# B step of a two-layer-type kernel: token rows of the queries turned by transposing DMAs, TensorE turning only the memory queries

## The chip, the core and the metric

One NeuronCore of one Trainium2 chip. The metric is the device time of one execution in microseconds (us), the time of that core. The kernel before was run three times: 2582.91, 2586.01 and 2589.53 us, median 2586.01 us.

## What is computed

Four residual layers run one after the other on a sequence of 2048 tokens of width 640: A, B, A, B, with a layer norm ahead of each. A is a segmented attention with a compressive memory and is not touched by the change. B is a recurrent attention with a memory of 8 rows, and its 64 segments of 32 tokens must be done in order, since the memory of a segment is what the segment before gave out:

```
mem = mem0                                             # 8 rows of 640
for s in range(64):                                    # segments of 32 tokens
    h = concat([mem, x[32*s : 32*s+32]])               # 40 rows
    q, k, v = h@Wq, h@Wk, h@Wv                         # 32 heads of 128
    scores = q@k.T / sqrt(128)                         # per head, 40 x 40
    scores = where((row < 8) | (row >= col), scores, -1e9)
    o = softmax(scores)@v @ Wo                         # 40 rows of 640
    mem = o[:8];  outs.append(o[8:])
```

## The kernel before, in words

A B layer is a loop of 64 steps (line 1089), one for each segment, with a setup ahead of it (lines 988 to 1038). All numbers in bf16, sums in fp32 in PSUM (the accumulation memory behind TensorE, which ScalarE and VectorE empty into SBUF).

**Which rows a step handles.** A step s projects 32 columns at once: the 8 memory rows of segment s, which have just been made by step s-1, and 24 token rows of segment s+1, which are known long before. So each of the projections gives 8 columns that are needed at once (by the scores of step s) and 24 that are kept for the next step. The other 8 token rows of a segment ("tails") are projected ahead in units of their own (`tail_unit`, `vtail_unit`), go through DRAM (`b_QKd`, `b_VTd`) and come back by DMA.

**The order of a step.** Every engine's order is written out by hand: `_OrdNC` (line 119) chains the instructions of TensorE, ScalarE, VectorE and GpSimd in the order of the program text. DMAs are issued by SyncE (SP), whose queue is in order too. The tile framework adds the semaphores: an instruction waits for whoever wrote what it reads, and for the readers and writers of the buffer that it takes over. In a step:

1. `thin_mm` (line 879) makes Ka, Qa, Kb, Qb: 16 heads each, 20 products, in PSUM as 128 rows (4 groups of heads by 32 columns) by 512. `kq` (line 1108) copies each to SBUF as bf16: Ka, Kb and Qb by ScalarE, Qa by VectorE (lines 1164 to 1171). The queries are scaled by SCB on the way.
2. These have to be turned, so that a head's 128 numbers lie along partitions. `transp4` (line 888) turns one 128 x 512 block by four TensorE transposes of 128 columns into a PSUM tile: TPak, TPaq, TPbk, TPbq (lines 1173 to 1183).
3. `scatter` (line 895) takes the 8 memory columns of each block by VectorE into this step's KT and QT, and `x_scatter` (line 1104) the 24 token columns by ScalarE into the next step's KT and QT. So VectorE does four copies of 128 x 128 and ScalarE four of 128 x 384.
4. `mask_mm` lays the mask into the score tiles SPa (ahead of TPbq) and SPb (behind it); `scores` (line 1119) then adds the products of 16 heads into SPa and of 16 into SPb, first with QT (the weights) and then with QZ (the tails' queries).
5. Softmax: row maxima, subtraction, sums and the normalization by VectorE (one half by GpSimd), exponentials by ScalarE; VectorE turns the probabilities (`p_turn`).
6. Beside the softmax TensorE makes Va, Vb and one tail unit; then the probability products (`pv`, tile b_OTP), the output projection (b_OPS, and a deferred part b_OPSd), a tail unit of V, and the eight new memory rows (b_MT) that VectorE puts into the next step's columns b_HX.

SyncE issues in a step two stores and two loads of the residual rows (b_XO, lines 1052 and 1102), a store of the tail unit (line 941), four loads of V tails (line 917), two stores of V tails (line 970), and in some steps a load of tails (line 907), of a layer norm's rows (line 848), and stores and loads of the deferred rows (lines 1061 and 1063).

In QT a head's 32 columns lie together: `QT[s][:, h, :]`, tokens first (0 to 23), memory rows last (24 to 31). The masks (`build_masks`, line 172) and the selection of the memory rows (`selm`) follow that order. The buffers b_kq (4) and b_QT (2) are used in turn.

Of the kernel before, what the change touches and what calls it, by code (L numbers as in the profile page):

```python
# [18 lines left out]
F32 = mybir.dt.float32  # L19
BF16 = mybir.dt.bfloat16  # L20
ACT = mybir.ActivationFunctionType
ALU = mybir.AluOpType
# [148 lines left out]

def build_masks(G, C, pool):

    G.tensor_tensor(out=C.selm[:, 0, :], in0=C.identb[:, 24:32], in1=C.identb[:, 88:96], op=ALU.add)
    G.tensor_tensor(out=C.selm[:, 1, :], in0=C.identb[:, 56:64], in1=C.identb[:, 120:128], op=ALU.add)
    G.memset(C.keep[:], 3e38)
    G.affine_select(out=C.keep[:], in_=C.keep[:], pattern=[[1, 128]], compare_op=ALU.is_ge, fill=0.0, base=0, channel_multiplier=-1)
    negs = pool.tile([128, 32], F32, name="b_negs", tag="am")
    G.memset(negs[:], -1e9)
    maskf = pool.tile([128, 2, 40], F32, name="b_maskf", tag="am")  # L180
    G.memset(maskf[:], 0.0)

    def above(out, rows, ncol, base, chan, colstep=1):
        G.affine_select(out=out, in_=negs[rows, 0:ncol], pattern=[[colstep, ncol]], compare_op=ALU.is_gt,
                        fill=0.0, base=base, channel_multiplier=chan)

    for i in range(4):
        r32 = slice(32 * i, 32 * i + 32)
        for k in (3, 2, 1, 0):
            rk = slice(32 * i, 32 * i + 8 * k + 8)  # L190
            above(maskf[rk, 0, 0:8], rk, 8, 8 * k, -1)
        above(maskf[r32, 1, 8:32], r32, 24, 0, -1)
        above(maskf[r32, 1, 0:8], r32, 8, 24, -1, 0)
    G.tensor_copy(C.mask5[:, 0, :], maskf[:, 0, :])
    G.tensor_copy(C.mask5[:, 1:5, :], maskf[:, 1, :].unsqueeze(1).to_broadcast([128, 4, 40]))

# [49 lines left out]
def layer_A(nc, tc, C, W, x_src, x_dst, src_is_bf16, nseg=4, out_bf16=False, xb_dst=None, load_w=None, side_loads=None):  # L246
# [7 lines left out]
    with ExitStack() as ctx:  # L254
# [367 lines left out]
        if src_is_bf16:  # L622
            build_masks(P, C, up)
# [154 lines left out]
def layer_B(nc, tc, C, W, x_src, xb_src, x_dst, mem0, B_Wv, B_Wo, nsteps=64, out_bf16=False, tag=""):  # L778
    SCB = 1.0 / math.sqrt(128.0)
    nc_raw = nc  # L780
    nc = _OrdNC(tc, nc_raw, engines=ORDER_ENGINES)
# [5 lines left out]
    with ExitStack() as ctx:  # L787
        def pool(name, bufs):
            return ctx.enter_context(tc.tile_pool(name=name, bufs=bufs, reuse_waits="tile"))
# [89 lines left out]
        def thin_mm(cols_ap, Wt, b, name):  # L879
            ps = ps_tile([128, 512], F32, name)  # L880
            for c in range(NCH):
                for j in range(4):
                    n = 4 * b + j
                    nc.tensor.matmul(ps[32 * j:32 * j + 32, :], lhsT=cols_ap[:, c, :], rhs=Wt[:, c, 512 * n:512 * n + 512],
                                     start=(c == 0), stop=(c == NCH - 1), tile_position=(0, 32 * j), skip_group_check=True)
            return ps

        def transp4(sb, name, tp=None):
            if tp is None:
                tp = ps_tile([128, 4, 128], BF16, name)  # L890
            for i in range(4):
                nc.tensor.transpose(tp[:, i, :], sb[:, 128 * i:128 * i + 128], C.identb[:])
            return tp

        def scatter(eng, tp, b, dst_t, t0, t1, c0):
            src = tp[:].rearrange("p i (j t) -> p i j t", j=4)[:, :, :, t0:t1]
            dst = dst_t[:, 16 * b:16 * b + 16, c0:c0 + (t1 - t0)].rearrange("p (j i) c -> p i j c", j=4)
            evac(eng, dst, src)

        def alloc_seg(s):  # L900
            QT[s] = w2.tile([128, 32, 32], BF16, name="b_QT", tag="QT")
            KT[s] = w2.tile([128, 32, 40], BF16, name="b_KT", tag="KT")

        def tails_load(s):
# [70 lines left out]
        def d_half(rows, jj2):  # L975
            return rows.rearrange("t (c j x) -> t j c x", j=2, x=64)[:, jj2]
# [36 lines left out]
        for nm, b in jobs:  # L1013
            ps = thin_mm(cols, W.wk if nm == "K" else W.wq, b, f"b_{nm}p")
            sb = kqp.tile([128, 512], BF16, name="b_kq", tag="kq")
# [4 lines left out]
        alloc_seg(0)  # L1020
        for (nm, b), sb in zip(jobs, sbs):
            tp = transp4(sb, "b_TP")
            scatter("dve" if nm == "K" else "act", tp, b, KT[0] if nm == "K" else QT[0], 8, 32, 8 if nm == "K" else 0)
        entered.append(1)
        XO, XOd = init_state()
        tl = tails_load(0)
# [22 lines left out]
        def store_head(s):  # L1049
            def f(xo):  # L1050
                for jj2 in range(2):
                    nc.sync.dma_start(d_half(x_dst[32 * s:32 * s + 24, :], jj2), xo[32 * jj2:32 * jj2 + 24, :].rearrange("t (c x) -> t c x", x=64))
            return f

        def tail_dma(s0, store, xo):
# [33 lines left out]
        for s in range(nsteps):  # L1089
            last = (s == nsteps - 1)  # L1090
# [8 lines left out]
                if s % 2:  # L1099
                    tl = tails_load(s + 1)  # L1100
            for jj2 in range(2):
                nc.sync.dma_start(XO[32 * jj2:32 * jj2 + 24, :].rearrange("t (c x) -> t c x", x=64), d_half(x_src[32 * s:32 * s + 24, :], jj2))

            def x_scatter(tp, b, D_):
                if not last:
                    scatter("act", tp, b, D_[s + 1], 8, 32, 8 if D_ is KT else 0)

            def kq(ps, eng, scale=None):
                sb = kqp.tile([128, 512], BF16, name="b_kq", tag="kq")
                evac(eng, sb[:], ps[:], scale)  # L1110
                return sb

            def mask_mm(b):
                SP = ps_tile([128, 5, 40], F32, f"b_SP{b}")
                nc.tensor.matmul(SP[:].rearrange("p g k -> p (g k)"), lhsT=C.identb[:], rhs=mask5[:].rearrange("p g k -> p (g k)"),
                                 start=True, stop=False, skip_group_check=True)
                return SP

            def scores(SPs):
                qz = QZ[:].rearrange("p h c -> p (h c)")  # L1120
                for b in range(2):
                    for tail in range(2):
                        for i in range(4):
                            for j in range(4):
                                h = 16 * b + 4 * j + i
                                lhsT = qz[:, 32 * h - 8 * i:32 * h - 8 * i + 32] if tail else QT[s][:, h, :]
                                nc.tensor.matmul(SPs[b][32 * j:32 * j + 32, 0 if tail else 1 + i, :], lhsT=lhsT, rhs=KT[s][:, h, :],
                                                 start=False, stop=True, tile_position=(0, 32 * j), skip_group_check=True)

# [37 lines left out]
            qa = kq(Qa, "dve", SCB)  # L1167
            Kb = thin_mm(cols, W.wk, 1, "b_Kb")
            kb = kq(Kb, "act")
            Qb = thin_mm(cols, W.wq, 1, "b_Qb")  # L1170
            qb = kq(Qb, "act", SCB)

            TPak = transp4(ka, "b_TPak")
            scatter("dve", TPak, 0, KT[s], 0, 8, 32)
            x_scatter(TPak, 0, KT)
            TPaq = transp4(qa, "b_TPaq")
            scatter("dve", TPaq, 0, QT[s], 0, 8, 24)
            x_scatter(TPaq, 0, QT)
            TPbk = transp4(kb, "b_TPbk")
            scatter("dve", TPbk, 1, KT[s], 0, 8, 32)  # L1180
            x_scatter(TPbk, 1, KT)
            SPa = mask_mm(0)
            TPbq = transp4(qb, "b_TPbq", po.tile([128, 4, 128], BF16, name="b_TPbq", tag="tail"))
            scatter("dve", TPbq, 1, QT[s], 0, 8, 24)
            x_scatter(TPbq, 1, QT)
            SPb = mask_mm(1)
            scores((SPa, SPb))
            for f in (soft_max, soft_sub, soft_exp):
# [59 lines left out]
            if not last:  # L1248
# [130 lines left out]
```

## Time and profile before

The profile is of one more execution.

| what | number |
|---|---|
| median of 3 runs | 2586.01 us |
| profiled execution, its own time | 2585.25 us |
| its span (first to last instruction) | 2583.5 us |
| granted TensorE clock over the span | 0.996 |
| a B step, from its first product of Ka to the next step's: median in the first B layer, in the second | 13.99, 13.97 us |
| shortest steps of both | 13.79 to 13.82 us |
| busy between 700 and 800 us of the span (first B layer): PE, PEld, DVE, ACT, POOL | 99.57, 64.95, 58.42, 52.09, 12.86 us |
| SP: time of its DMA issues in a step, mean of 56 steps of the first B layer | 9.76 us |

PE is TensorE's products, PEld its weight loads, DVE VectorE, ACT ScalarE, POOL GpSimd, SP SyncE's queue. A row of the timeline has the start in us from the span's start, the time in us, the engine, the line, the operation, the tiles (out<-in), the shape and how many were merged; in brackets the idle time ahead of it and what ended it. Nearly all rows of a B step carry line 109, since the helper that records the order makes the call; they are told apart by their tiles. A PE row's end is modelled, and the rows overlap, so that a PE that looks busy can still have waited.

### The profile page before, as it was taken

To read this page: it belongs to the slowest core of one execution; us is meant where nothing else is said; L and a number is where in the kernel's file an instruction comes from. 1 tells how busy PE (TensorE), PEld (TensorE's weight loads), DVE (VectorE), ACT (ScalarE), POOL (GpSimd) and SP (SyncE) were. 2 spreads that over 40 slices of the span, in tenths; PEclk is the share of its full clock that TensorE was granted. 3 is DMA by queue.
4 is the path that set the end of the run, shared out by engine and by line. 5 is a ranking of instruction groups with operands and counts; after the bars stand their busy time and mean duration, and the time that the engine had idled before them with its cause. 6 is when DMAs were issued, how large, how long until landed. Compare 5 with 4: busy or idle time off the path is not lost.

```text
span 2583.5 us, 139561 instructions
## 1 busy us (share of the span) xinstructions
PE 2482.8 (96%) x62024; PEld 1637.5 (63%) x62088; DVE 1704.5 (66%) x4738; ACT 1521.3 (59%) x3430; POOL 704.9 (27%) x1515
## 2 busy tenths in 40 slices
PE   7999999999999999999979899999999999999998
PEld 5556576666666666666655566766666666666665
DVE  8999855565556555555579998555655565565555
ACT  6988945555555545444369889455555555555443
POOL 6677621111111111111146776211111111111110
PEclk9999999999999999999999999999999999999999
DMA  4122272222222222121220112822212122211111
GB/s 158 45 84 73 83 245 51 48 47 46 46 50 48 46 50 43 40 39 30 61 85 17 63 50 55 265 47 47 44 42 47 42 46 43 46 43 35 38 26 21
DMA packets 325309, 157.19 MB, mean 61 GB/s; under 512 B 244960, under 2 KB 309600, under 8 KB 322912
## 3 DMA queue, kind: packets, MB, share of 16 engines
q1 hardware_dynamic: 324704, 148.26, 22.1%
q8 instruction: 485, 7.95, 1.3%
q14 instruction: 120, 0.98, 0.1%
HBM read 96.46 MB, written 51.71 MB: 57 GB/s over the span
## 4 chain that ended last, share of the span: by engine, by line
PE 77%; DVE 14%; ACT 6%; issue 2%; DMA 1%; POOL 0%; SPq 0%; ACTq 0%; DVEq 0%; POOLq 0%
PE b_OPS L109 11%; DVE a_nm L138 6%; PE b_Ka L109 5%; PE b_Qb L109 5%; PE b_Kb L109 5%; PE b_Qa L109 5%; PE b_tail L109 5%; PE b_SP L109 4%; PE b_Va L109 4%; PE b_Vb L109 4%; PE b_vtail L109 3%; PE b_OPSd L109 3%; ACT a_PT L138 3%; PE b_OTP L109 3%; PE a_S L109 2%
## 5 line engine op out<-in xcount | busy, mean ns | idle before, releaser
L109 PEld LDWEIGHTS <-b_HX 128*32 128x32 bf16 x15360 | 428.7, 96 | 329.5 <-DVE b_HX L109 0.5
L109 POOL TENSOR_TENSOR b_Pn<-b_E,b_rs 128x200 bf16<-128x200 bf16 x128 | 78.2, 611 | 1334.4 <-PE b_Vb L109 893.7
L138 DVE TENSOR_REDUCE a_nm<-a_S 128x2 f32<-128x512 f32 (+3 forms) x512 | 395.0, 816 | 34.7 <-PE a_S L109 26.4
L138 ACT ACTIVATE a_PT<-a_T 128x1024 bf16<-128x1024 f32 (+1 forms) x384 | 344.3, 901 | 32.8 <-PE a_T L109 25.0
L109 PE MATMUL b_OPS<-b_wo,b_OTsb 128*32 128x320 bf16 x8192 | 302.4, 299 | 1.8 <-issue 0.8
L109 PEld LDWEIGHTS <-b_OTsb 128*32 128x32 bf16 x8192 | 204.4, 96 | 77.2 <-DVE b_OTsb L109 3.1
L138 POOL TENSOR_SCALAR_AFFINE_SELECT a_PT<-a_PT 128x256 bf16<-128x256 bf16 x380 | 188.6, 505 | 129.8 <-ACT a_PT L138 128.4
L109 DVE CAST b_HX<-b_MT 128x8 bf16<-128x8 f32 x372 | 63.9, 172 | 232.3 <-PE b_MT L109 226.6
L109 ACT CAST b_msb<-b_OPS 128x64 bf16<-128x64 f32 x378 | 69.4, 256 | 222.1 <-PE b_OPS L109 222.0
L109 ACT CAST b_kq<-b_Kb 128x512 bf16<-128x512 f32 x128 | 75.0, 586 | 200.4 <-PE b_Kb L109 200.4
L109 DVE COPY b_KT<-b_TPak 128x128 bf16<-128x128 bf16 x128 | 28.8, 225 | 228.1 <-PE b_TPak L109 228.1
L109 DVE TENSOR_SCALAR b_kq<-b_Qa 128x512 bf16<-128x512 f32 x128 | 88.6, 692 | 120.0 <-PE b_Qa L109 116.7
L109 PE MATMUL b_Va<-b_wv,b_HX 128*32 128x512 bf16 x2520 | 161.1, 380 | 0.0
L109 PE MATMUL b_Vb<-b_wv,b_HX 128*32 128x512 bf16 x2520 | 160.9, 379 | 0.0
L109 PEld LDWEIGHTS <-b_kq 128*128 128x128 bf16 x2080 | 116.8, 98 | 68.9 <-ACT b_kq L109 55.6
L109 PE MATMUL b_Ka<-b_wk,b_HX 128*32 128x512 bf16 x2520 | 158.3, 378 | 0.0
L109 PE MATMUL b_Qa<-b_wq,b_HX 128*32 128x512 bf16 x2520 | 158.2, 379 | 0.0
L109 PE MATMUL b_Qb<-b_wq,b_HX 128*32 128x512 bf16 x2520 | 158.2, 379 | 0.0
L109 PE MATMUL b_Kb<-b_wk,b_HX 128*32 128x512 bf16 x2520 | 158.2, 379 | 0.0
L109 DVE CAST b_OTsb<-b_OTP 128x160 bf16<-128x160 f32 (+1 forms) x384 | 131.0, 377 | 35.0 <-PE b_OTP L109 28.9
L109 PEld LDWEIGHTS <-c_identb 128*128 128x128 bf16 x1240 | 102.2, 98 | 60.1 <-issue 29.4
L109 ACT CAST b_kq<-b_Ka 128x512 bf16<-128x512 f32 x128 | 75.0, 586 | 108.8 <-PE b_Ka L109 108.8
(206 smaller groups left out, 5502.4 us busy)
## 6 DMA issues: line engine op xcount, KB each, us to landing
b_QKd<-b_tu SPq DMA_DIRECT2D x128, 128.0 KB
b_tl<-b_QKd SPq DMA_DIRECT2D x64, 256.0 KB
b_wv<-in_B_Wv_dram SPq DMA_DIRECT2D x10, 1024.0 KB
b_wo<-in_B_Wo_dram SPq DMA_DIRECT2D x16, 640.0 KB
b_Vth<-b_VTd SPq DMA_DIRECT2D x512, 16.0 KB
b_XO<-xres SPq DMA_DIRECT2D x256, 30.0 KB
b_VTd<-b_vt SPq DMA_DIRECT2D x224, 32.0 KB
b_xt<-xres_bf SPq DMA_DIRECT2D x40, 160.0 KB
```

The source lines that it names most:

```text
L109: r = f(*a, **k)
L138: r = f(*a, **k)
```

## The change

In a step, the 24 token rows of the queries no longer come from a TensorE transpose and a copy by ScalarE. Two transposing DMAs, issued by SyncE, turn all 128 x 512 of qa and of qb straight from b_kq into the next step's QT. TensorE turns only the 8 memory columns of each 32: `mem_turn` makes products with b_kq as weights and a strided view of the identity (4 runs of 8 columns, 32 columns a product) into fp32 PSUM, and VectorE copies these 128 x 128 numbers into this step's QT. ScalarE's two copies of the token queries go. Qb is emptied from PSUM in two halves, by ScalarE and by VectorE. QT's layout becomes `[128, 2, 4, 128]`, with the memory columns first in each 32; masks, selection and the partitions of the residual rows (8 to 31 in place of 0 to 23) follow. K stays as it was. The setup makes the first QT as before, in the new layout. In the last step there is no next QT and no DMA, but the halves and `mem_turn` stay.

```
+        def mem_turn(sb, b, name, tp=None):
+            if tp is None:
+                tp = ps_tile([128, 4, 32], F32, name)
+            for i in range(4):
+                nc.tensor.matmul(tp[:, i, :], lhsT=sb[:, 128 * i:128 * i + 128], rhs=C.identb[:].rearrange("p (j t) -> p j t", t=32)[:, :, 0:8],
+                                 start=True, stop=True, skip_group_check=True)
+            return tp
+
+        def q_cols(s, b, t0, t1):
+            return QT[s][:, b, :, :].rearrange("p i (j t) -> p i j t", t=32)[:, :, :, t0:t1]
...
-            QT[s] = w2.tile([128, 32, 32], BF16, name="b_QT", tag="QT")
+            QT[s] = w2.tile([128, 2, 4, 128], BF16, name="b_QT", tag="QT")
...
-                nc.sync.dma_start(XO[32 * jj2:32 * jj2 + 24, :].rearrange("t (c x) -> t c x", x=64), d_half(x_src[32 * s:32 * s + 24, :], jj2))
+                nc.sync.dma_start(XO[32 * jj2 + 8:32 * jj2 + 32, :].rearrange("t (c x) -> t c x", x=64), d_half(x_src[32 * s:32 * s + 24, :], jj2))
...
-                                lhsT = qz[:, 32 * h - 8 * i:32 * h - 8 * i + 32] if tail else QT[s][:, h, :]
+                                lhsT = qz[:, 32 * h - 8 * i:32 * h - 8 * i + 32] if tail else QT[s][:, b, i, 32 * j:32 * j + 32]
...
-            qb = kq(Qb, "act", SCB)
+            qb = kqp.tile([128, 512], BF16, name="b_kq", tag="kq")
+            evac("act", qb[:, 0:256], Qb[:, 0:256], SCB)
+            evac("dve", qb[:, 256:512], Qb[:, 256:512], SCB)
+            if not last:
+                for b, sb in ((0, qa), (1, qb)):
+                    nc.sync.dma_start_transpose(out=QT[s + 1][:, b, :, :], in_=sb[:])
...
-            TPaq = transp4(qa, "b_TPaq")
-            scatter("dve", TPaq, 0, QT[s], 0, 8, 24)
-            x_scatter(TPaq, 0, QT)
+            TPaq = mem_turn(qa, 0, "b_TPaq")
+            evac("dve", q_cols(s, 0, 0, 8), TPaq[:].rearrange("p i (j t) -> p i j t", t=8))
...
-            TPbq = transp4(qb, "b_TPbq", po.tile([128, 4, 128], BF16, name="b_TPbq", tag="tail"))
-            scatter("dve", TPbq, 1, QT[s], 0, 8, 24)
-            x_scatter(TPbq, 1, QT)
+            TPbq = mem_turn(qb, 1, "b_TPbq", po.tile([128, 4, 32], F32, name="b_TPbq", tag="tail"))
+            evac("dve", q_cols(s, 1, 0, 8), TPbq[:].rearrange("p i (j t) -> p i j t", t=8))
```

More of the change, by code (lines that the diff above doesn't have):

```diff
@@ L172, in build_masks @@
 def build_masks(G, C, pool):
-    G.tensor_tensor(out=C.selm[:, 0, :], in0=C.identb[:, 24:32], in1=C.identb[:, 88:96], op=ALU.add)
-    G.tensor_tensor(out=C.selm[:, 1, :], in0=C.identb[:, 56:64], in1=C.identb[:, 120:128], op=ALU.add)
+    G.tensor_tensor(out=C.selm[:, 0, :], in0=C.identb[:, 0:8], in1=C.identb[:, 64:72], op=ALU.add)
+    G.tensor_tensor(out=C.selm[:, 1, :], in0=C.identb[:, 32:40], in1=C.identb[:, 96:104], op=ALU.add)
     G.memset(C.keep[:], 3e38)
@@ L191, in build_masks @@
             above(maskf[rk, 0, 0:8], rk, 8, 8 * k, -1)
-        above(maskf[r32, 1, 8:32], r32, 24, 0, -1)
-        above(maskf[r32, 1, 0:8], r32, 8, 24, -1, 0)
+        above(maskf[r32, 1, 8:32], r32, 24, 8, -1)
+        G.memset(maskf[r32, 1, 0:8], -1e9)
+        G.memset(maskf[32 * i:32 * i + 8, 1, :], 0.0)
     G.tensor_copy(C.mask5[:, 0, :], maskf[:, 0, :])
@@ L1022, in layer_B @@
             tp = transp4(sb, "b_TP")
-            scatter("dve" if nm == "K" else "act", tp, b, KT[0] if nm == "K" else QT[0], 8, 32, 8 if nm == "K" else 0)
+            if nm == "K":
+                scatter("dve", tp, b, KT[0], 8, 32, 8)
+            else:
+                evac("act", q_cols(0, b, 8, 32), tp[:].rearrange("p i (j t) -> p i j t", t=32)[:, :, :, 8:32])
         entered.append(1)
@@ L1051, in f @@
                 for jj2 in range(2):
-                    nc.sync.dma_start(d_half(x_dst[32 * s:32 * s + 24, :], jj2), xo[32 * jj2:32 * jj2 + 24, :].rearrange("t (c x) -> t c x", x=64))
+                    nc.sync.dma_start(d_half(x_dst[32 * s:32 * s + 24, :], jj2), xo[32 * jj2 + 8:32 * jj2 + 32, :].rearrange("t (c x) -> t c x", x=64))
             return f
@@ L1101, in layer_B @@
             for jj2 in range(2):
-                nc.sync.dma_start(XO[32 * jj2:32 * jj2 + 24, :].rearrange("t (c x) -> t c x", x=64), d_half(x_src[32 * s:32 * s + 24, :], jj2))
+                nc.sync.dma_start(XO[32 * jj2 + 8:32 * jj2 + 32, :].rearrange("t (c x) -> t c x", x=64), d_half(x_src[32 * s:32 * s + 24, :], jj2))
             def x_scatter(tp, b, D_):
                 if not last:
-                    scatter("act", tp, b, D_[s + 1], 8, 32, 8 if D_ is KT else 0)
+                    scatter("act", tp, b, D_[s + 1], 8, 32, 8)
             def kq(ps, eng, scale=None):
```

## The prediction

> **What bounds the kernel now.** I read the page first: the busy shares and the chain of work that ended last.
>
> ```profile
> PE 2482.8 (96%) x62024; PEld 1637.5 (63%) x62088; DVE 1704.5 (66%) x4738; ACT 1521.3 (59%) x3430; POOL 704.9 (27%) x1515
> PE 77%; DVE 14%; ACT 6%; issue 2%; DMA 1%; POOL 0%; SPq 0%; ACTq 0%; DVEq 0%; POOLq 0%
> ```
>
> TensorE is the bound, so its saved columns look like time. But PE's ends are modelled, so I then read the timeline where the change sits: all engines, 814.9 to 817.3 us, a step of the first B layer.
>
> ```profile
> 815.09 0.40 PE L109 MATMUL b_TPak<-c_identb,b_kq 128*128 128x128 bf16 x4
> 815.27 0.60 ACT L109 ACTIVATE b_kq<-b_Qb 128x512 bf16<-128x512 f32 x1 [0.50 <-PE b_Qb L109]
> 815.33 0.39 PE L109 MATMUL b_TPaq<-c_identb,b_kq 128*128 128x128 bf16 x4
> 815.53 0.23 DVE L109 COPY b_KT<-b_TPak 128x128 bf16<-128x128 bf16 x1 [1.78 <-PE b_TPak L109]
> ...
> 815.75 0.22 DVE L109 COPY b_QT<-b_TPaq 128x128 bf16<-128x128 bf16 x1
> ...
> 815.93 0.40 PE L109 MATMUL b_TPbq<-c_identb,b_kq 128*128 128x128 bf16 x4
> 815.97 0.23 DVE L109 COPY b_KT<-b_TPbk 128x128 bf16<-128x128 bf16 x1
> ...
> 816.36 0.23 DVE L109 COPY b_QT<-b_TPbq 128x128 bf16<-128x128 bf16 x1 [0.16 <-PE b_TPbq L109]
> ...
> 816.64 0.28 PE L109 MATMUL b_SP<-b_KT,b_QT 128*32 128x40 bf16 x16
> ...
> 816.83 0.83 DVE L109 TENSOR_REDUCE b_negmax<-b_SP 128x5 f32<-128x200 f32 x2 [0.24 <-PE b_SP L109]
> ```
>
> Qb's last product ends at 815.16 (modelled), ScalarE starts to empty it 0.11 later and is done at 815.87; only then TPbq; VectorE's last copy ends at 816.585; 0.054 later (median of 128 steps) the second 16 heads' scores start. Behind them in PE's order stands Va (816.86), and VectorE's second row maximum waits for them too. So **the end of VectorE's fourth copy starts the rest of the step on both engines**; until then TensorE has idle time that the 96% hides. Steps are 13.98 us (median), the shortest 13.8; TensorE or the softmax ends later by turns, and a delay of that copy moves both.
>
> Last, the groups by shape, for VectorE over the span and for ScalarE from 400 to 1290 us (after the bar: busy us, mean ns of one).
>
> ```profile
> L109 DVE TENSOR_SCALAR b_kq<-b_Qa 128x512 bf16<-128x512 f32 x128 | 88.6, 692 | 120.0 <-PE b_Qa L109 116.7
> L109 DVE CAST b_OTsb<-b_OTP 128x160 bf16<-128x160 f32 x256 | 80.2, 325 | 35.0 <-PE b_OTP L109 28.9
> L109 DVE CAST b_HX<-b_MT 128x16 bf16<-128x16 f32 x248 | 43.2, 175 | 6.0 <-PE b_MT L109 0.4
> L109 DVE COPY b_QT<-b_TPbq 128x128 bf16<-128x128 bf16 x128 | 28.8, 225 | 20.6 <-PE b_TPbq L109 19.9
> L109 DVE CAST b_OTdef<-b_vtail 128x256 bf16<-128x256 f32 x8 | 3.4, 425 | 4.6 <-PE b_vtail L109 4.6
> L109 DVE COPY b_KT<-b_TP 128x384 bf16<-128x384 bf16 x4 | 1.2, 348 | 0.0
> ```
>
> ```profile
> L109 ACT ACTIVATE b_kq<-b_Qb 128x512 bf16<-128x512 f32 x63 | 37.6, 597 | 31.7 <-PE b_Qb L109 30.9 <-PE b_TPak L109 0.8
> L109 ACT CAST b_kq<-b_Kb 128x512 bf16<-128x512 f32 x63 | 36.9, 586 | 98.5 <-PE b_Kb L109 98.5
> L109 ACT CAST b_vt<-b_vtail 128x256 bf16<-128x256 f32 x55 | 20.5, 372 | 29.7 <-ACT b_msb L109 26.5 <-issue 2.2 <-PE b_vtail L109 0.9
> ```
>
> From PSUM VectorE takes 1.04 ns a column in fp32 (256 columns 425, 512 692) but 0.48 in bf16 (128 columns 225, 384 348).
>
> **The change part by part.**
>
> *Qb in two halves.* The diff reads as if ScalarE and VectorE ran side by side. The instruction order of the changed program says otherwise: VectorE's half waits for ScalarE's semaphore, at the count that ScalarE's half of the same step raises (same PSUM tile, same SBUF tile). So the halves run in turn. ScalarE: 372 for 256 columns, plus 11 that an ACTIVATE takes over a CAST (597 - 586), 0.383 us. Hand-over: 0.033 (ScalarE's exponential to VectorE's sum, median). VectorE: 0.425 (the fp32 row of 256 columns; at 512 the scaled form takes what a cast takes, 692). So qb is whole at 815.27 + 0.383 + 0.033 + 0.425 = 816.11, not 815.87. Worse, this half stands in VectorE's order **ahead of its four copies**, three of which ran while ScalarE still emptied Qb.
>
> *The four copies.* Two stay (K, 0.225 each). The two of the memory queries now read fp32: between 175 at 16 columns and 325 at 160, 128 columns give 0.292. No row has this exact form; the ends are 0.225 (what the bf16 copy took) and 0.325. I take 0.292. Together 1.034, back to back: from 816.11 to 817.145, against 816.585. **The delay is 0.56 us a step.** All that they read is ready: TPbq's last two products start at about 816.16, when the half is done, and end within 0.3, while VectorE comes to the copy at 816.85.
>
> *TensorE's narrower products.* Eight products of 128 columns at 0.056 each (0.225 from one group of four to the next) become 32 columns. The trace has no 128-row weights with so few columns. Bounds: no gain (the weight load sets the pace), or 0.009 each (32 b_OTP products in 0.30), so 0 to 0.38 us a step. I count 0: TensorE then waits for VectorE's copies, which cover it whole. If that cover were gone, the start of the scores would still be VectorE's, not TensorE's.
>
> *ScalarE's two copies* (0.484 and 0.509 us) go. I count 0: its next work, the exponential, waits for VectorE's subtraction (0.94 idle ahead of it in this step); that wait grows.
>
> *The transposing DMAs.* Their order in SP's queue: qa behind the two stores of b_XO and ahead of its loads, qb behind the loads, ahead of the tail store (L941) and the V tails' loads (L917). Two things wait for them: the next step's copies into b_kq and its scores. The former is due 13 us after the issue of qa's, so even late landings cost nothing there. Of the issue:
>
> ```profile
> L1102 SPq DMA_DIRECT2D b_XO<-xres x256: 762/782/4413, 381.3 to 2564.8; - x128
> ```
>
> ```profile
> L941 SPq DMA_DIRECT2D b_QKd<-b_tu x128: 319/373/2332, 359.2 to 2334.6; - x128
> ```
>
> No transposing DMA is in the trace. Ends: 0.32 (the store of 128 partitions, 128 KB, the same bytes), and 4.41 (the longest b_XO load, with a wait in it). I take 0.78, the median of the b_XO loads, which move short pieces as the transposes do. SP issues 9.76 us a step; with two it is 11.3 of 14.54. Cost 0 below 2.39 us each, (14.54 - 9.76)/2. What is moved back behind them by 1 to 2 us (tail store, V tails) is used in the next step, over 8 us later.
>
> [...]
>
> *The rest at 0*: masks (eight small GpSimd writes for four, once, beside layer A, where GpSimd has idle time; at most 2 us); QT's layout (the scores' weights are 32 adjoining columns as before); b_XO's partitions (same shapes).
>
> **The sum.** The halves and copies are in all 64 steps of both layers: 128 x 0.56 = 71.7. The profiled execution took 2585.25 (span 2583.5 and 1.75 around it), so 2656.9, forecast **2657 us** (+2.8%); the runs' median is 0.76 above that execution, which I leave.
>
> **The rivals.**
>
> *SP becomes the bound.* For it: SP is 70% full, and every step would wait for it once an issue takes over 2.39. At 4.41 a step is 9.76 + 8.82 = 18.58, 4.6 over now, in 126 steps 580: 3165 us. Against it: every clean issue row is under 0.9.
>
> *The halves do run side by side* (were the wait for an older count). VectorE starts at about 815.21 and ends its copies at 815.21 + 0.425 + 1.034 = 816.67, 0.085 late: +11 us, 2596. Against it: the count.
>
> *Not slower: side by side and short copies.* If VectorE empties its half beside ScalarE and its memory copies cost less than 0.25 each, the last copy comes earlier than now. At 0.225 it ends at 816.535, 0.05 early: -6 us, 2579. For it: 0.225 is this very copy's row. Against it: the count, and both fp32 rows. Above 0.25 it turns into the rival before.
>
> **How the numbers follow.** Forecast 0.83; SP bound 0.07; side by side 0.04; side by side with short copies 0.04 (no change: a measurement here tells 0.3%, 8 us, from none); 0.02 for a gain that I see no mechanism for. Slower 0.94, same 0.04, faster 0.02. Range: memory copies at 0.225 give 0.426 x 128 = 55, 2640; at 0.325, 80, 2665. Some steps may also wait for a transpose behind a full SP queue (the steps with deferred rows, one in four; 0.8 us in each of 32 is 26). So 2636 to 2688; SP as the bound is left out.
>
> **What would show it.** Right: VectorE's b_kq<-b_Qb starts 0.03 after ScalarE's ends, five VectorE instructions stand back to back, memory copies at 0.29, Va 0.56 later against Qb, TensorE's idle time grows there, steps of 14.5. Wrong: VectorE's half beside ScalarE's; copies at 0.22; SP rows above 2.4, or VectorE, PE waiting for b_QT's DMA. A step in which TensorE overtakes the delay (steps under 14.2) would say that the fourth copy was not what starts the rest.

## The result, and the profile after

The changed kernel took 2624.94 us (median of 4 runs, 2620.51 to 2627.21) against 2586.32 for the kernel before (4 runs, 2582.91 to 2589.53): 1.0148 times, 95% interval [1.0133, 1.0164]. So it is slower by 38.6 us, about half of the 71.7 forecast, and below the range of 2636 to 2688. The profiled execution took 2627.21 us, its span is 2625.5.

The engines' and the chain's lines of the page after:

```profile
PE 2484.5 (95%) x62024; PEld 1634.2 (62%) x62088; DVE 1729.9 (66%) x4866; ACT 1408.3 (54%) x3178; POOL 705.1 (27%) x1519
PE 74%; DVE 12%; ACT 7%; DMA 3%; issue 2%; SPq 0%; POOL 0%; ACTq 0%; DVEq 0%
```

ScalarE has lost 113 us of work, VectorE has gained 25, and TensorE, whose eight turning products of the queries got narrower in each step, is as busy as before. The chain's share of DMA is 3% for 1%: in single steps it leads through a DMA into the products of P x V, but the stretch of the step in which these waits would lie did not grow (3.904 before, 3.899 after, third column of the table below).

The place of the change, in a step of the first B layer (timeline of the changed kernel: start, us, engine):

```profile
825.32 0.38 ACT L109 ACTIVATE b_kq<-b_Qb 128x256 bf16<-128x256 f32 x1 [0.49 <-PE b_Qb L109]
...
825.73 0.42 DVE L109 TENSOR_SCALAR b_kq<-b_Qb 128x256 bf16<-128x256 f32 x1 [1.93 <-ACT b_kq L109]
...
826.08 0.21 DVE L109 COPY b_KT<-b_TPak 128x128 bf16<-128x128 bf16 x1
826.21 0.28 DVE L109 CAST b_QT<-b_TPaq 128x128 bf16<-128x128 f32 x1
...
826.40 0.21 DVE L109 COPY b_KT<-b_TPbk 128x128 bf16<-128x128 bf16 x1
826.53 0.28 DVE L109 CAST b_QT<-b_TPbq 128x128 bf16<-128x128 f32 x1
...
827.24 1.27 PE L109 MATMUL b_Va<-b_wv,b_HX 128*32 128x512 bf16 x20
```

VectorE's half waits 1.93 us, until ScalarE's half is out; then five VectorE instructions stand in a row. Look at the starts: the second is 0.35 behind the first, though the first takes 0.42, and the fourth copy starts 0.45 behind the first copy, though three copies ahead of it take 0.21 + 0.28 + 0.21 = 0.70. Each starts before the one ahead of it has ended.

For all that follows I cut each step at four events and took means over 126 steps of both B layers (us, worked out from the traces; the step runs from its first product of Ka to the next step's). P x V are the products of the probabilities with the values. Each row is one profiled execution:

| kernel | Ka to first score | to Va | to 2nd half of P x V | to last b_MT | step |
|---|---|---|---|---|---|
| before | 5.672 | 0.542 | 3.904 | 3.783 | 14.031 |
| after | 5.821 | 0.578 | 3.899 | 3.957 | 14.383 |
| e1 | 5.545 | 0.602 | 3.900 | 3.965 | 14.139 |
| e2 | 5.809 | 0.542 | 3.890 | 3.799 | 14.169 |
| e3 | 5.822 | 0.580 | 3.895 | 3.911 | 14.337 |
| e4 | 5.754 | 0.558 | 3.931 | 3.836 | 14.207 |
| e5 | 5.825 | 0.573 | 3.894 | 3.844 | 14.261 |
| e6 | 5.551 | 0.594 | 3.906 | 3.858 | 14.033 |
| e7 | 5.680 | 0.541 | 3.902 | 3.885 | 14.133 |
| e8 | 5.678 | 0.547 | 3.906 | 3.806 | 14.065 |
| e9 | 5.613 | 0.554 | 3.909 | 3.796 | 14.001 |
| e10 | 5.417 | 0.595 | 3.940 | 3.903 | 13.988 |
| e11 | 5.404 | 0.594 | 3.915 | 3.896 | 13.940 |
| e12 | 5.923 | 0.534 | 3.883 | 3.837 | 14.471 |

After less before: 0.149 + 0.036 = 0.185 us up to Va, the place that the prediction spoke of, and **0.174 us in the last stretch**, the output projection, where nothing was changed. Times 126 that is 23.3 and 21.9 us; the stretch between the layers gave back 3.1. The prediction had the first (at three times its size) and not the second. The last stretch is not sharp: before, e2 and e8, which have the same waits on TensorE, lie within 0.023 of each other, and after and e3, whose median times agree, 0.046 apart.

**What the second is.** The groups of products of the output projection (behind the bar: busy us, mean ns of one; behind the second bar the idle time ahead of them and what ended it), before and then after:

```profile
L109 PE MATMUL b_OPS<-b_wo,b_OTsb 128*32 128x320 bf16 x8192 | 302.4, 299 | 1.8 <-issue 0.8 <-DVE b_OTsb L109 0.5 <-ACT b_OTsb L109 0.4
L109 PE MATMUL b_OPSd<-b_wo,b_OTdef 128*32 128x320 bf16 x2048 | 115.3, 302 | 2.1 <-issue 1.9
```

```profile
L109 PE MATMUL b_OPS<-b_wo,b_OTsb 128*32 128x320 bf16 x8192 | 305.8, 299 | 9.1 <-issue 8.1 <-DVE b_OTsb L109 0.6
L109 PE MATMUL b_OPSd<-b_wo,b_OTdef 128*32 128x320 bf16 x2048 | 116.8, 302 | 6.8 <-issue 6.7
```

"issue" is time in which the engine waits for nothing that the profile shows; it has grown from 2.7 to 14.8 us. One of these stalls in the timeline of the changed kernel; the products stop inside a group whose operands are all there:

```profile
918.46 2.29 PE L109 MATMUL b_OPS<-b_wo,b_OTsb 128*32 128x320 bf16 x59
...
921.88 0.43 PE L109 MATMUL b_OPS<-b_wo,b_OTsb 128*32 128x320 bf16 x5 [1.13 <-issue]
921.88 0.10 PEld L109 LDWEIGHTS <-b_OTsb 128*32 128x32 bf16 x4 [1.46 <-issue]
```

The missing thing, as I read it, is the instructions themselves. The page has a DMA queue of kind "instruction" with 486 packets and 7.96 MB in the span, 16 KB each:

```profile
q8 instruction: 486, 7.96, 1.3%
```

There are as many packets as 256 instructions in each would give: the program has 124,581 TensorE instructions, 486.6 times 256 (before 124,235, 485.3 times, and 485 packets). When I counted the instructions of the program up to each stall over 0.6 us from the output projection on (25 after, 5 before), all but one fell on the same place: number 193 or 194 modulo 256, the first instruction of a new packet, and ended 1.1 to 1.8 us after that packet's transfer did. From these counts and times I take it that TensorE ran out of instructions; no row shows it as such. A step whose border falls badly loses 0.65 us on the mean.

"Badly" is a border on the 704th to 767th instruction of the step: 29 of 128 steps before, 35 after. So the number of such steps hardly grew; what each loses did, from 0.22 to 0.65 us (the mean of its last stretch less about 3.72 us, which is near the median of the other steps before).

### The profile page after: what moved, and what is told of

It reads as the page before. It is cut to its first block, busy times and chain, and to the rows that moved or that the text cites. A ratio compares the mean times of both kernels' runs of the same rounds, so it can differ in the third digit from the quotient of the medians.

```text
span 2625.5 us, 140236 instructions
## 1 busy us (share of the span) xinstructions
PE 2484.5 (95%) x62024; PEld 1634.2 (62%) x62088; DVE 1729.9 (66%) x4866; ACT 1408.3 (54%) x3178; POOL 705.1 (27%) x1519
## 3 DMA queue, kind: packets, MB, share of 16 engines
q8 instruction: 486, 7.96, 1.3%
## 4 chain that ended last, share of the span: by engine, by line
PE 74%; DVE 12%; ACT 7%; DMA 3%; issue 2%; SPq 0%; POOL 0%; ACTq 0%; DVEq 0%
PE b_OPS L109 11%; PE b_tail L109 7%; PE b_Va L109 5%; PE b_Vb L109 5%; PE b_Ka L109 5%; DVE a_nm L138 5%; PE b_Qa L109 5%; PE b_Kb L109 4%; PE b_Qb L109 4%; PE b_SP L109 4%; PE b_vtail L109 3%; PE b_OTP L109 3%; PE b_OPSd L109 3%; ACT a_PT L138 3%; PE a_S L109 2%
## 5 line engine op out<-in xcount | busy, mean ns | idle before, releaser
L109 PEld LDWEIGHTS <-b_HX 128*32 128x32 bf16 x15360 | 440.2, 96 | 322.5 <-DVE b_HX L109 1.7
L109 DVE TENSOR_SCALAR b_kq<-b_Qb 128x256 bf16<-128x256 f32 x128 | 54.3, 425 | 247.4 <-ACT b_kq L109 237.7
L109 PEld LDWEIGHTS <-b_kq 128*128 128x128 bf16 x2080 | 105.0, 97 | 96.5 <-ACT b_kq L109 55.5
L109 ACT ACTIVATE b_E<-b_SP 128x200 bf16<-128x200 f32 x256 | 75.6, 338 | 133.7 <-DVE b_SP L109 133.5
L109 PE MATMUL b_vtail<-b_wv,b_TX 128*32 128x256 bf16 x2880 | 135.6, 271 | 4.1 <-issue 4.0
```

Of the source, the lines that this page charges most:

```text
L109: r = f(*a, **k)
```

## The experiments

In e1 to e4 three theories of the loss in the last stretch stand against each other: A, the added transposing DMAs hold TensorE's instruction fetches back; B, TensorE's added instructions and the place of the borders do it; C, the split of Qb does it.

**e1: no split** (ScalarE empties the whole of Qb, all else as in the changed kernel).

```
-            qb = kqp.tile([128, 512], BF16, name="b_kq", tag="kq")
-            evac("act", qb[:, 0:256], Qb[:, 0:256], SCB)
-            evac("dve", qb[:, 256:512], Qb[:, 256:512], SCB)
+            qb = kq(Qb, "act", SCB)
```

> The changed kernel with Qb emptied by ScalarE alone, as before; transposing DMAs and narrow products stay. Theory A (two terms: VectorE's half and the copies behind it start the scores 0.175 us later in each step, 22 us in all; the transposing DMAs delay TensorE's instruction stream, 16 us): the last copy of the memory queries then starts at 5.55 us of the step instead of 5.69, since the narrow TPbq ends earlier, and ends 0.08 earlier than before, -10 us; the stalls stay, +16; so about 2592 us. Rival B (the stalls come from where the chunks of TensorE's instructions fall, three more waits a step, not from the DMAs): the same 2592, this run does not tell them apart. Rival C (all 38 us come from VectorE's half): 2576 us.

Measured: 2596.01 us, 1.0032 [1.0020, 1.0043] times before. The first score comes 0.127 us earlier than before the change, the last stretch is as long as in the changed kernel (3.965). C falls. And the split costs 0.0116 of 2586 by the two ratios, 30 us: all of the loss up to Va and more.

**e2: the split alone**, put into the kernel before (the three lines of e1 the other way round).

> The kernel before with one edit of the change alone: Qb emptied in two halves, by ScalarE and then VectorE. Theory A: the half ends at 5.43 us of the step, TPbq's last two transposes at 5.78, the last VectorE copy at 6.02 instead of 5.91, 0.11 us a step, about 2600 us, and TensorE stalls as rarely as before (three of more than 0.6 us in the first B layer). Rival C (the half is the whole loss): 2625 us. If the five VectorE instructions ran one after the other without overlap, as the prediction had it (0.425 and four of 0.225), the copy would end at 6.34: 0.43 a step, 2640 us.

Measured: 2604.69 us, 1.0064 [1.0049, 1.0078]. The fourth copy starts 0.134 us later, Va 0.134 later (medians), the last stretch stays (3.799). 126 x 0.134 = 17 us, and 0.0064 of 2586, 16.6, were measured: here the end of VectorE's fourth copy does carry the step one for one.

**e3: plain DMAs** in the transposes' place, same buffers and bytes; the token queries stay unturned, so the numbers computed are others.

```
-                    nc.sync.dma_start_transpose(out=QT[s + 1][:, b, :, :], in_=sb[:])
+                    nc.sync.dma_start(QT[s + 1][:, b, :, :], sb[:].rearrange("p (i x) -> p i x", x=128))
```

> The changed kernel with plain DMAs in the place of the transposing ones: the same bytes from the same tiles to the same tiles, the same waits, but not turned, so that the token rows of the queries are left unturned. Theory A (the transposing DMAs delay TensorE's instruction stream): the stalls fall to the three or so per layer of before, about 2609 us. Rival B (place of the chunks; the instructions of TensorE are the same, 817.7 a step): nine or so stalls per layer stay, 2625 us. SP's issue of each falls from 1.25 us to about 0.35 in either case.

Measured: 2624.38 us, 1.0138 [1.0124, 1.0151], as the change. Issues (ns, min/median/max), of the changed kernel and of e3:

```profile
L1191 SPq DMA_TRANSPOSE b_QT<-b_kq x252: 1188/1246/2632, 395.4 to 2595.6; - x126
```

```profile
L1191 SPq DMA_DIRECT2D b_QT<-b_kq x252: 532/552/1622, 395.6 to 2588.6; - x126
```

The plain issue took 0.55 us, not 0.35 as expected. Half the issue time and no transposing changes nothing in the median time: it is not the turning.

**e4: the transposes alone**, added to the kernel before behind the scores, into the b_QT buffer just read; nobody uses what they write.

```
             scores((SPa, SPb))
+            if not last:
+                for b, sb in ((0, qa), (1, qb)):
+                    nc.sync.dma_start_transpose(out=QT[s][:].rearrange("p h c -> p (h c)")[:, 512 * b:512 * b + 512].rearrange("p (i x) -> p i x", x=128), in_=sb[:])
```

> The kernel before with the transposing DMAs added, two a step, of qa and qb into the query tile that has just been read for the last time; nothing reads what they write. TensorE's instructions are exactly those of before (814.9 a step). Theory A: stalls as in the changed kernel, +16 us, about 2602 us. Rival B (place of the chunks): as before, 2586 us. If the queue of SP is what costs time (two issues of 1.25 us a step more), a wait of VectorE, ScalarE or TensorE for a DMA shows up in the trace.

Measured: 2615.25 us, 1.0101 [1.0083, 1.0119], more than either theory gave. The trace has a cost that the changed kernel does not have. SP's transposes in one place of the timeline, the load of b_XO that SP issues behind them, and the next copies into b_kq, which the prediction had named as waiting for the transposes:

```profile
1033.26 3.03 SPq L1190 DMA_TRANSPOSE b_QT<-b_kq  x2
...
1036.34 1.73 SPq L1102 DMA_DIRECT2D b_XO<-xres  x1
...
1038.29 0.40 PE L109 MATMUL b_TPak<-c_identb,b_kq 128*128 128x128 bf16 x4
...
1039.21 0.60 ACT L109 ACTIVATE b_kq<-b_Qb 128x512 bf16<-128x512 f32 x1 [1.30 <-DMA b_QT<-b_kq]
1039.75 1.01 DVE L109 TENSOR_TENSOR b_XO<-b_OPS,b_XO 64x320 f32<-64x320 f32 x2 [5.59 <-DMA b_XO<-xres]
...
1040.79 0.69 DVE L109 TENSOR_SCALAR b_kq<-b_Qa 128x512 bf16<-128x512 f32 x1
...
1041.54 0.40 PE L109 MATMUL b_TPaq<-c_identb,b_kq 128*128 128x128 bf16 x4 [2.85 <-DVE b_kq L109]
```

ScalarE's copy of Qb waited 1.30 us for a transpose that still read its buffer; there are 6 such waits, 8.7 us in all. VectorE's copy of Qa stands in its order behind the b_XO addition, which waited 5.59 us for the load issued behind the transposes; there are 18 such waits, 38.1 us in all (3 of 1.4 us in all in the changed kernel). In 11 steps Qa's eviction comes 0.4 to 4.5 us behind its median time, and the scores with it. In the changed kernel it is never over 0.14 late. So e4 is no clean test, but the last stretch (3.836) says that the DMAs alone bring about a third of the loss there (0.053 of 0.174), not much more than executions differ by.

**What e1 to e4 left**: the loss is there in after, e1 and e3 and hardly in before, e2 and e4. The first three share more than that. TensorE waits in them for the DMAs into b_QT by two separate instructions a step, ahead of the first and of the second 16 heads' scores (252 in all, none before); no run takes these two away and leaves the rest alone. And they share a wait that lies closer to the loss. In the built program of the change no weight load and no product of TensorE carries more than one wait (7,782 of 124,176 carry one); a third wait stands ahead of the two as an instruction of its own. The first product of P x V, before and after (number in the step, instruction, what it waits for):

```
before  443 Ldweights  b_Vth         a DMA
        444 Matmult    b_OTP         VectorE (b_PTa)
after   445 EventSemaphore           VectorE (b_PTa)
        446 Ldweights  b_Vth         a DMA
        447 Matmult    b_OTP         ScalarE (b_KT<-b_TPbk: the buffer's last reader)
```

Before, ScalarE was the last reader of b_TPbq, so the tail unit, which takes over that buffer, waited for ScalarE and covered the third wait; 32 steps had the separate wait all the same. After, VectorE is its only reader, and 126 steps have it. The third wait is long fulfilled; but it pushes the wait that is really open, that for the softmax, into an instruction of its own. Theory W, my guess: TensorE reads on past a product that waits, but not past a separate wait, and so asks too late for its next 256 instructions. The kernel before is a test by itself: among its steps with a border on the 704th to 767th instruction, the 6 with the separate wait lose 0.585 us, the 23 without it 0.120. (The 32 steps are one in four and not a random choice; without such a border they are 0.065 us longer too. But in the changed kernel the others have the wait as well, and the 27 of them with such a border lose 0.647.)

**e5: the changed kernel with one separate wait less**: a ScalarE read of one column of b_TPbq.

```
+            rd = sm.tile([128, 1], BF16, name="b_rd", tag="rd")
+            evac("act", rd[:], TPbq[:, 0, 0:1])
```

> The changed kernel with one more ScalarE instruction a step: it reads one column of b_TPbq. By that TensorE has seen ScalarE's count before it comes to the first P x V product, and the separate wait instruction ahead of that product goes in 94 of its 126 steps (32 keep it, as in the kernel before); 124,487 TensorE instructions for 124,581. Theory W (the separate wait holds TensorE's instruction stream back, so that the next 256 instructions are asked for too late): steps in which a border of 256 instructions falls on the 704th to 767th lose 0.65 us now and 0.2 to 0.3 then, 35 of 128; the stretch from the second half of P x V to the last b_MT goes from 3.96 to 3.83 mean; 2607 to 2612 us. Rival T (the added DMA traffic, or the number of instructions, delays the fetches): 2625, and the stretch stays at 3.95. The read itself is off the path in both (ScalarE idles there); if not, up to 0.2 us a step more.

**e6: e1 with the same read.**

> e1 (the whole of Qb's eviction on ScalarE, all else as in the changed kernel) with the same read. W: 2596 less 14 to 18, so 2578 to 2582, below the kernel before. T: 2596 as e1.

**e7: the kernel before with the separate wait in 126 steps**, by an exchange of two buffers.

```
-            TPbk = transp4(kb, "b_TPbk")
+            TPbk = transp4(kb, "b_TPbk", po.tile([128, 4, 128], BF16, name="b_TPbk", tag="tail"))
-            TPbq = transp4(qb, "b_TPbq", po.tile([128, 4, 128], BF16, name="b_TPbq", tag="tail"))
+            TPbq = transp4(qb, "b_TPbq")
```

> The kernel before with the banks of two transposes exchanged (b_TPbk takes the bank of b_tail, b_TPbq a common one): no work is added or taken, no DMA either, but the separate wait ahead of the first P x V product is there in 126 steps instead of 32. W: the loss of steps whose border falls on the 704th to 767th instruction goes from 0.22 to 0.6 us, the stretch from 3.78 to 3.88, the kernel to 2597 to 2602. T: 2586 to 2589, as before.

**e8: the kernel before with e5's read**, which changes none of its waits.

> The kernel before with the one-column ScalarE read of e5 added, which changes none of its separate waits (32 steps): the price of the read alone. Both theories: as before within 0.2% (ScalarE idles 0.9 us ahead of the exponential); if the read were on the path, 0.2 us x 126 = 25 us more, and e5 and e6 would have to be read against that.

| kernel | us | times before, interval | steps with separate wait | loss of a step with border at 704-767: with it, without | last stretch |
|---|---|---|---|---|---|
| before | 2586.95 | | 32 | 0.585 (6 steps), 0.120 (23) | 3.783 |
| after | 2624.94 | 1.0148 | 126 | 0.652 (35), none | 3.957 |
| e5 | 2615.20 | 1.0119 [1.0103, 1.0135] | 32 | 0.610 (6), 0.164 (23) | 3.844 |
| e6 | 2585.33 | 0.9994 [0.9985, 1.0003] | 32 | 0.440 (6), 0.180 (23) | 3.858 |
| e7 | 2595.12 | 1.0035 [1.0023, 1.0048] | 126 | 0.487 (30), none | 3.885 |
| e8 | 2586.16 | 0.9994 [0.9985, 1.0003] | 32 | 0.427 (6), 0.199 (23) | 3.806 |

The ratios are those on record with the runs, which are not exactly the quotients of these medians. The number of separate waits decides in both directions: by the ratios, taking 94 away gives 7.5 us back (e5 against after) and 9.8 (e6 against e1), putting them in costs 9.1 (e7), and the read itself costs nothing (e8). By the intervals these are known to some 6, 4 and 3 us, an estimate. So the rival T falls. But the sizes lie under the 13 to 18 expected of e5 and e6, and e7 just under its range. In e5 and e6 the borders moved as well, 29 bad steps for 35; at 0.65 us each that is 4 us of the gain. The groups of e5 and of e7, to set beside those of after (8.1 and 6.7 of "issue") and before (0.8 and 1.9):

```profile
L109 PE MATMUL b_OPS<-b_wo,b_OTsb 128*32 128x320 bf16 x8192 | 304.6, 299 | 4.1 <-issue 3.0 <-DVE b_OTsb L109 0.3
L109 PE MATMUL b_OPSd<-b_wo,b_OTdef 128*32 128x320 bf16 x2048 | 115.2, 302 | 2.6 <-issue 2.6
```

```profile
L109 PE MATMUL b_OPS<-b_wo,b_OTsb 128*32 128x320 bf16 x8192 | 303.8, 299 | 5.5 <-issue 4.5 <-DVE b_OTsb L109 0.6
L109 PE MATMUL b_OPSd<-b_wo,b_OTdef 128*32 128x320 bf16 x2048 | 115.1, 302 | 3.7 <-issue 3.6
```

The fetch is seen to start later, too: in the steps with a bad border it starts 0.91 us (mean) behind the first product of P x V before, in those without the separate wait, and 1.40 after; 1.12 in e5 without it (1.48 in its 7 steps with it), 1.32 in e7. Against it stands that in the 6 steps before with the wait the fetch starts at 0.99, hardly later, though they lose 0.585. That the instruction reader stops at a separate wait is inferred; no row of the trace shows it. What is shown is that the waits cost the time.

**e9, e10, e11: Qb in two PSUM tiles**, to move the fourth copy the other way. The 20 products of 512 columns become 40 of 256, the first half is emptied while TensorE still fills the second:

```
+            for x in range(2):
+                Qx = ps_tile([128, 256], F32, "b_Qb")
+                for c in range(NCH):
+                    for j in range(4):
+                        w0 = 512 * (4 + j) + 256 * x
+                        nc.tensor.matmul(Qx[32 * j:32 * j + 32, :], lhsT=cols[:, c, :], rhs=W.wq[:, c, w0:w0 + 256],
+                                         start=(c == 0), stop=(c == NCH - 1), tile_position=(0, 32 * j), skip_group_check=True)
+                evac(ENG, qb[:, 256 * x:256 * x + 256], Qx[:], SCB)
```

e9 is the kernel before with that, ENG always ScalarE; e10 is e6 with it; e11 is e10 with VectorE emptying the second tile.

> The kernel before, but Qb's 20 products of 512 columns become 40 of 256 into two PSUM tiles, and ScalarE empties them one after the other; the first is whole while TensorE still fills the second. Nothing else of the change. So qb is whole 0.2 us earlier (its second half takes 0.383 behind Qb's end, not 0.597), and b_TPbq and VectorE's fourth copy follow it. Theory A (the end of the fourth copy starts the rest of the step on both engines, in both directions): last copy from 5.69 to 5.50 behind the step's start, Va from 6.19 to 6.00, 0.19 x 126 = 24 us less, 2562. Rival R (a step can't get shorter by that: TensorE's products or the softmax are the limit): 2584 to 2588. Rival N (the narrow products cost TensorE more): Qb's end moves from 4.49 to 4.6 or later, and the gain is halved or gone.

> e6 (transposing DMAs, narrow memory products, Qb on ScalarE, the extra read) with Qb in two PSUM tiles, both emptied by ScalarE. A: last copy from 5.54 to 5.35, 2585 less 24, so 2561, no better than e9: the transposing DMAs bring nothing that the two tiles don't. If SP's queue (12.4 us of issues in a step of 13.85) is the limit: VectorE's b_kq<-b_Qa comes late in more than the 7 steps of e6, 2570 to 2590.

> As e10, but VectorE empties the second tile: now the halves can overlap, since they lie in two PSUM tiles (in the changed kernel they lay in one, and VectorE waited for ScalarE). VectorE's half starts at 4.6 instead of 5.01, its fourth copy at 4.6 + 0.80 = 5.40 (0.80 from half to fourth copy as in the changed kernel) instead of 5.81: 0.41 x 126 = 52 us less than the changed kernel without the separate wait (2615), 2563. If the wait was not what cost time there: 2600 or more.

Measured: 2577.87 us, 0.9971 [0.9960, 0.9983]; 2578.62 us, 0.9969 [0.9959, 0.9979]; 2577.63 us, 0.9976 [0.9966, 0.9986] times before (2586.34 in these runs). All three are a little faster than both kernels, none by the 24 us expected; e11 is 37.6 us under e5 where 52 were expected. In e9 the fourth copy moved only 0.064 us, since TensorE's own row of turning products (one group of four each 0.223) now comes last; Va moved 0.063, and 126 x 0.063 = 8 us is what came out. In e10 and e11 the copy moved 0.318 us (median) and Va 0.20 to 0.22 (mean), 25 to 27 us; 0.12 x 126 = 15 are lost again in the last stretch (bad borders without the separate wait cost 0.25 now), and Qa's eviction is late in 15 and 9 steps, as in e4. In e11 the two halves no longer wait for each other (timeline):

```profile
813.41 0.38 ACT L109 ACTIVATE b_kq<-b_Qb 128x256 bf16<-128x256 f32 x1
813.91 0.42 DVE L109 TENSOR_SCALAR b_kq<-b_Qb 128x256 bf16<-128x256 f32 x1 [1.48 <-PE b_Qb L109]
```

VectorE's half waits for TensorE, no longer for ScalarE, though both still write one SBUF tile: in the change it was the common PSUM tile that put them in turn. Side by side they still do not run, since ScalarE has ended when TensorE gives the second tile out; the half starts 4.55 us into the step for 5.01 in the change.

**e12: no DMAs**: e5 with a GpSimd fill of b_QT in their place; the token queries are left out.

```
-                for b, sb in ((0, qa), (1, qb)):
-                    nc.sync.dma_start_transpose(out=QT[s + 1][:, b, :, :], in_=sb[:])
+                nc.gpsimd.memset(QT[s + 1][:], 0.0)
```

> e5 (the changed kernel with the read that takes 94 separate waits away) without any DMA for the token queries: one GpSimd fill with zeros of the next step's b_QT in their place, so the token queries are left out. VectorE's chain is as in e5. It asks what is left of the loss beyond that chain (Va 0.18 us later, 126 x 0.18 = 23 us) and the separate waits: the stretch from the second half of P x V to the last b_MT is 3.84 mean in e5 and 3.78 in the kernel before. Theory D (the added DMAs themselves hold TensorE's instruction fetches or the evictions back): the stretch returns to 3.78 and the time to 2587 + 23 = 2608 to 2610. Rival E (they cost nothing; the rest is the same in both or lies with the order of the instructions): 2615 and 3.84, as e5.

Measured: 2638.73 us, 1.0193 [1.0178, 1.0207], outside both. The fill brought a cost of its own. VectorE's normalization of a layer norm's rows in e5 and in e12 (first B layer), and the fill:

```profile
L109 DVE TENSOR_SCALAR b_xt<-b_xt,b_ln_mv,b_ln_rstd 128x640 bf16<-128x640 bf16 x16 | 7.9, 493 | 10.7 <-POOL b_ln_rstd L109 10.7
```

```profile
L109 DVE TENSOR_SCALAR b_xt<-b_xt,b_ln_mv,b_ln_rstd 128x640 bf16<-128x640 bf16 x16 | 22.1, 1383 | 10.7 <-POOL b_ln_rstd L109 10.7
```

```profile
L109 POOL MEMSET b_QT<- 128x1024 bf16 x126 | 120.0, 952 | 0.0
```

The normalization takes 1383 ns beside the fill instead of 493, and b_HX, which stands behind it, comes over 0.5 us late in 27 steps, which the time between the last b_MT and the next step shows (0.292 us mean for 0.124). The 890 ns that it takes longer are near the 952 of a fill, and in the timeline the two overlap: the normalization runs from 824.54 to 825.92 us, the fill from 824.80 to 825.75. What holds VectorE up there no row shows. The last stretch stays at e5's length in the mean (3.837 for 3.844), so the DMAs do not show as the cause of what is left there, but since the first score comes 0.1 later too and 23.5 us of new cost lie around it, I do not call that shown. The equal means also hide a difference: the steps without a bad border take 3.769 us there, 3.805 in e5 and 3.741 before, so that a part of it may be theirs.

## Why the prediction was wrong, step by step

- **The halves run in turn**: right, to 0.01 us. VectorE's half starts 0.033 us behind ScalarE's end and ends 5.43 us into the step, forecast 5.44. e2 and e11 show it from both sides. One reading beside it was wrong: of the copies before, two, not three, ran while ScalarE still emptied Qb (they start at 815.53 and 815.75, the third at 815.97, and ScalarE ends at 815.87).
- **"Together 1.034, back to back"**: this step failed. The durations were right: 0.214 and 0.280, forecast 0.225 and 0.292. But they don't add. In the changed kernel each copy starts 0.083 us (median of 512) before the end of the VectorE instruction ahead of it, so that the four copies took 0.656 us behind the half. The last copy ends 0.175 later than before (6.087 for 5.912), not 0.56, and Va starts 0.177 later. The row was there in the profile of before: one subtraction takes 365 ns by its group, and two in a row 0.64. That 38.6 us came out, half of the forecast and not a third, is luck: this step alone gives 22 to 23, and a cost that the prediction did not have makes up the rest.

```profile
L109 DVE TENSOR_TENSOR b_SP<-b_SP,b_negmax 128x200 f32<-128x200 f32 x256 | 81.8, 365 | 0.5 <-DVE b_SP L109 0.4 <-DVE b_negmax L109 0.2
```

```profile
817.58 0.64 DVE L109 TENSOR_TENSOR b_SP<-b_SP,b_negmax 128x200 f32<-128x200 f32 x2
```

  What misled me: before, the copies started 0.22 apart and lasted 0.225, which looked like VectorE's pace. It was TensorE's, whose groups of four transposes came 0.223 apart.
- **"The end of the fourth copy starts the rest of the step"**: right. The shift of Va is that of the copy in after (0.177 for 0.175), e2 (0.134 for 0.134) and e9 (0.063 for 0.064). In e10 and e11 it no longer sets all of it.
- **Narrower products at 0**: right as a cost on the path; they do run faster, one each 0.026 us instead of 0.056, and TensorE waits that time away. In e1, without the split, they count: VectorE waits 0.134 us (mean) ahead of the fourth copy there, which ends 0.077 earlier than before, and the first score comes 0.127 earlier.
- **ScalarE's two copies at 0**: as a time, right. But what went with them was ScalarE's place as last reader of b_TPbq, and that is the second thing that failed: a dependency that was removed brought 94 separate waits more (126 for 32) and with them 7 to 14 us (7.5, 9.8 and 9.1 by the runs; 0.113 x 126 by e5's stretch). The prediction counted waits by who ends last, not by how many stand on an instruction.
- **The transposing DMAs at 0**: the issue takes 1.25 us, not 0.78, and SP's issues fill 12.4 us of the step (forecast 11.3); the threshold of 2.39 was far (3 of 252 issues lie above it). TensorE waited for these DMAs to land 3 times, 0.5 us in all. The transposes do move pieces as short as those of b_XO: before, the trace has 61,440 packets of 256 bytes, as many as the 384 moves of b_XO (30 KB) and the 96 of b_XOd and b_XOe (40 KB) give; after, 190,464, which is 512 more for each of the 252 transposes. Yet their issue takes 1246 ns where that of the b_XO loads takes 787. e3 shows that it costs the kernel nothing whether the DMA turns (2624.94 us, and 2624.38 in e3), though SP's issue took 1246 ns for 552 with a plain DMA. The sum "26 us for steps behind a full queue" came to nothing in after and to much in e4; nor do the range's ends follow from its terms (2665 + 26 is 2691, not 2688, and nothing leads from 2640 to 2636).
- **The rivals**: SP as the bound and the halves side by side did not happen. Nothing foresaw the instruction fetches.

The account of the 38.6 us (42.0 between the two profiled executions): some 23 by the later scores and Va (0.185 x 126), 7 to 14 by the separate waits; between the layers 3 come back. What is left of the last stretch, about 0.06 us a step or 8 us, stays open: e5, e6 and e12 have it, each with 32 separate waits ahead of P x V as before. They still have separate waits ahead of the scores, two a step in e5 and e6 and one in e12, and none before; whether these are the cause was not tested. And e8, which has none of them, lies 0.023 above before as well, so that some of the 0.06 may be the difference between executions.

## What to carry to other kernels

Add up starts, not durations: find two instructions of the engine in a row without a wait and take their distance; and ask of a regular distance whose it is. When a reader of a buffer changes engine, look at the built order for a wait that has become an instruction of its own: here 94 more of them went with 7 to 14 us, where TensorE had waited for the softmax and then ran 256 instructions in 2.7 to 3.5 us. A place that is "issue" in the profile and jumps from step to step can be the instruction stream: count the instructions modulo the packet (29 of the 30 stalls counted here lay at 193 or 194 modulo 256).

## What the runs showed of the hardware

- TensorE's instructions come in packets of 16 KB, 256 each (486 packets for 124,581 instructions). In the steps with a bad border TensorE runs a packet's 256 instructions in 2.7 to 3.5 us when nothing holds it. The transfer of the next one starts 1.2 us after the first of them (median after; 0.9 before) and takes 0.9 to 1.5, and at the stalls the first instruction follows 1.1 to 1.8 after its end. Together that is 3.2 to 4.5 us after, an estimate from these figures: mostly too late.
- Steps with a bad border and a separate wait ahead of P x V lost 0.2 to 0.5 us more than those with the border alone (0.585 against 0.120 before, 0.610 against 0.164 in e5, 0.440 against 0.180 in e6, 0.427 against 0.199 in e8).
- Turning products of 128 rows by 32 columns follow each other at 0.026 us (b_TPaq after), those of 128 columns at 0.056 (before).
- Beside GpSimd's fill of 952 ns VectorE's bf16 instruction of 493 ns (e5) lasted 1383 (e12).
